# Where GpSimd issues the first two blocks of w_in in a fused attention and feed-forward kernel

## The chip, the cores and the metric

The kernel runs on one core of a Trainium2 chip. The metric is the device time of one execution in microseconds (us); a lower time is better. The core has a matrix engine (TensorE, in the profile PE, with its weight loads as PEld), VectorE (DVE), ScalarE (ACT), GpSimd (POOL) and SyncE (SP, which here only issues DMAs). GpSimd computes and also issues DMAs, in the order of its own instruction stream.

## The reference

Cosine attention over 8 batches of 12 heads, 448 positions and head size 64, followed by a two-layer network with an exact GELU:

```python
q_n = q / (np.linalg.norm(q, axis=-1, keepdims=True) + 1e-06)
k_n = k / (np.linalg.norm(k, axis=-1, keepdims=True) + 1e-06)
scores = np.matmul(q_n, k_n.transpose(0, 1, 3, 2)) / tau
scores = scores - np.max(scores, axis=-1, keepdims=True)
attn = np.exp(scores)
attn = attn / (np.sum(attn, axis=-1, keepdims=True) + 1e-09)
attn_out = np.matmul(attn, v)
...
x = attn_out.transpose(0, 2, 1, 3).reshape(B * S, H * D)
h = x @ w_in
g = 0.5 * h * (1.0 + erf(h * inv_sqrt2))
return g @ w_out
```

`x` is 3584 x 768, `w_in` 768 x 2048, `w_out` 2048 x 768. All inputs are float32 in DRAM; the products run in bf16.

## The kernel before

Heads are handled in quads of four: 24 quads in all, three for each batch. A quad's Q and K are loaded by `load_qk(g)` into one tile `qk` (four buffers), 448 KB for each of Q and K, on SP's queue. Quad 0 is split in two half quads, and so the work before the scores goes by units: unit 0 and unit 1 are the halves of quad 0, unit 2 is quad 1, unit 3 is quad 2, and so on.

For a unit u, `square` makes the squares (ScalarE for the first units, GpSimd later), `reduce` sums them on VectorE, `logs` and `roots` make the norms on ScalarE, `inverses` makes the reciprocals `rn` on VectorE, and `scale(u)` multiplies Q and K by them on GpSimd into the bf16 tile `qkb`. `transposes(u, i)` turns Q or K on TensorE, and `copies` moves the result to `qkT` on VectorE. Then, per quad, `scores` (TensorE), `exps` (ScalarE), `sums` of the exponentials (TensorE), `values` (TensorE, reads V) and `normalise` (VectorE), which writes the quad's columns of `x`.

V and both weights are loaded by GpSimd, whose DMAs turn float32 into bf16 on the way. `load_v(0)` brings quad 0's V, `load_v(1)` that of quads 1 and 2. `load_wi(i)` brings a block of `w_in`, as two DMAs, one for each half of the partitions: blocks 0 and 1 hold the rows that quads 0 and 1 meet, all columns; blocks 2 and 3 are the two column halves of the rows for quad 2. `load_wo(i)` brings a quarter of `w_out`. All of these go through one DMA queue (q0 in the profile); SP's loads and stores go through another (q1).

The first batch is written out by hand in `opening()`: there is no planner, and each engine works through its instructions in the order in which the calls stand there. `opening()` calls `load_wi(0)` behind `roots(0)`, ahead of `scale(0)`, and `load_wi(1)` behind `roots(2)`, ahead of `scale(2)`. GpSimd's stream up to the first squares is therefore: a one-element copy that waits for quad 0 (`late_copy`), load_v(0), load_wi(0), scale(0), scale(1), load_v(1), load_wi(1), scale(2), scale(3) Q, load_wi(2), scale(3) K, load_wi(3), squares of units 4 and 5, load_wo(0), load_wo(1). TensorE uses block 0 first in `mm(0, 4, 0, 2)`, between the last values of quad 2, then blocks 0 and 1 in `mm(0, 2, 0, 4)` and what follows, then blocks 2 and 3 in the products that finish each bank. `spin` issues products whose result nobody reads.

Of the kernel before, what the change touches and what calls it, by code (L numbers as in the profile page):

```python
# [16 lines left out]
def kernel(  # L17
# [109 lines left out]
    def load_qk(g, queue=None):  # L127
        b, n = divmod(g, NQ)
        t = qkp.tile([128, 2, 2, C, D], F32, tag="qk", name=f"qk{g}")
        qk_t[g] = t  # L130
        for s0, s1 in ((0, 1), (1, 2)) if g == 0 else ((0, 2),):
            for i, src in enumerate((q, k)):
                eng = queue or (nc.scalar if g == 0 and s0 == 0 and i == 1 else nc.sync)
                eng.dma_start(  # L134
                    out=t[:, i, s0:s1].rearrange("p s c d -> p s (c d)"),
                    in_=src[b, 4 * n + 2 * s0:4 * n + 2 * s1].rearrange(
                        "(s h) (p c) d -> (h p) s (c d)", h=2, c=C))
# [14 lines left out]
    def square(u, parts=None):  # L152
        g, s0, s1 = units[u]
        for eng, i in parts or ((nc.gpsimd, 0), (nc.gpsimd, 1)):
            if (g, i) not in sq_t:
                sq_t[g, i] = sqp.tile([128, 2, C, D], F32, tag="sq", name=f"sq{g}_{i}")
            sq, t = sq_t[g, i][:, s0:s1], qk_t[g][:, i, s0:s1]
            if eng is nc.scalar:
                eng.activation(sq, t, AF.Square)  # L159
            else:  # L160
                eng.tensor_tensor(sq, t, t, ALU.mult)  # L161
# [16 lines left out]
    def roots(n):  # L178
        ln = ln_t.pop(n)
        sr_t[n] = root2[2 if len(groups[n]) == 2 else n % 2][:, :math.prod(shapes[n])]  # L180
        nc.scalar.activation(sr_t[n][:, :, 0], ln.rearrange("p j i s c -> p (j i s c)"), AF.Exp, scale=0.5)
# [15 lines left out]
    def scale(u, parts=None):  # L197
        g, s0, s1 = units[u]
        n, j = place[u]
        rn = rn_t[n][:, j]  # L200
        if g not in qkb_t:
            qkb_t[g] = qkbp.tile([128, 2, C, 2, D], BF16, tag="qkb", name=f"qkb{g}")
        qkb, t = qkb_t[g], qk_t[g]
        for eng, i in parts or ((nc.gpsimd, 0), (nc.gpsimd, 1)):
            eng.tensor_tensor(  # L205
                qkb[:, i, :, s0:s1].rearrange("p c s d -> p s c d"), t[:, i, s0:s1],
                rn[:, i].to_broadcast([128, s1 - s0, C, D]), ALU.mult)
# [3 lines left out]
    def transposes(u, i=None):  # L211
        g, s0, s1 = units[u]
        qkb = qkb_t[g]
        if g not in qkT_t:
            qkT_t[g] = qkTp.tile([128, 2, C, 128], BF16, tag="qkT", name=f"qkT{g}")
        if i is None:
            nc.sync.dma_start_transpose(out=qkT_t[g].rearrange("p i c s -> p (i c) s"),
                                        in_=qkb.rearrange("p i c s d -> p (i c s d)"))
            return
        tp = tp_t[u, i] = mm_tile(f"tp{u}_{i}", (128, C, 128), BF16)  # L220
        for c in range(C):
            nc.tensor.transpose(tp[64 * s0:64 * s1, c, :], qkb[:, i, c, s0:s1].rearrange("p s d -> p (s d)"), ident)  # L222
# [10 lines left out]
    def scores(g, banks, p=None):  # L233
        qkT = qkT_t[g]
        if p is None:
            p = st_turn[0]
            st_turn[0] ^= 1
        st = pair(p, f"st{g}_{banks[0][1]}")
        for n, (s, c) in enumerate(banks):
            rows = slice(64 * s, 64 * (s + 1))  # L240
            for h in range(2):
                cols = slice(64 * h, 64 * (h + 1))
                nc.tensor.matmul(st[cols, n, :S], lhsT=qkT[rows, 1, c, cols], rhs=qkT[rows, 0, :, cols],  # L243
                                 start=True, stop=True, tile_position=(64 * s, 64 * h))
        st_t[g, banks[0]] = st

    def exps(g, banks):
        st = st_t.pop((g, banks[0]))
        if g not in all_t:
            all_t[g] = ptp.tile([128, C, 2, S], BF16, tag="pt", name=f"pt{g}")  # L250
        (s0, c0), (s1, c1) = banks
        pt = all_t[g][:, c0] if c0 == c1 else all_t[g][:, c0:c1 + 1, s0]
        nc.scalar.activation(pt, st[:, :, :S], AF.Exp, scale=inv_tau)  # L253
        for n, (s, c) in enumerate(banks):
            pt_t[g, s, c] = pt[:, n]
# [192 lines left out]
    def load_wi(i):  # L448
        n = min(i, NQ - 1)
        half = d_ff // 2  # L450
        cols = slice(0, d_ff) if n < NQ - 1 else slice((i - n) * half, (i - n + 1) * half)
        for s in range(2):
            nc.gpsimd.dma_start(
                out=wi[64 * s:64 * (s + 1), 2 * n:2 * n + 2, cols],
                in_=moe_w_in[:, cols].rearrange("(n s h d) f -> n s d h f", s=2, h=2, d=D)[n, s])
# [16 lines left out]
    def spin(n):  # L472
        ps = ps_mm.tile([128, 512], F32, tag=f"mm{turn[0]}", name="spin")
        for _ in range(n):
            nc.tensor.matmul(ps[:, :S], lhsT=ident, rhs=blank, start=True, stop=True)
# [48 lines left out]
    def opening():  # L524
# [14 lines left out]
        logs(0)  # L539
        reduce(1, Q)  # L540
        roots(0)
        load_wi(0)
        square(1, ((AC, K),))
        inverses(0)
        square(2, ((AC, Q),))
# [15 lines left out]
        copies(0, 0)  # L561
        square(3, ((AC, K),))
        scale(1, ((GP, 1),))
        load_qk(4)
        spin(1)
        transposes(1, 0)
# [5 lines left out]
        logs(2)  # L572
        scores(0, ((0, 2), (0, 3)))
        roots(2)
        load_wi(1)
        exps(0, ((0, 0), (0, 1)))
        inverses(2)
        copies(1, 1)
# [10 lines left out]
        spin(1)  # L589
        scores(0, ((1, 2), (1, 3)))  # L590
        scale(2, ((GP, 1),))
        load_qk(5)
        transposes(2, 0)
        exps(0, ((1, 2), (1, 3)))
# [763 lines left out]
    def open_fourth():  # L1358
        single.close()
        late[3] = ctx.enter_context(tc.tile_pool(name="ps_fourth", bufs=1, space=bass.MemoryType.PSUM))  # L1360

    opening()
    assert not todo_t, len(todo_t)
    first(2)
# [40 lines left out]
```

## Time and profile before

| what | us |
|---|---|
| runs of the kernel before | 392.3, 392.84, 399.61 |
| median | 392.84 |
| profiled execution | 393.7 |
| its span, first to last instruction | 391.9 |
| GpSimd busy | 246.9 |
| ScalarE busy | 270.3 |
| VectorE busy | 273.8 |

The span is what the profile shows; the profiled execution's own time holds 1.8 us around it. Times in rows are microseconds from the start of the span. A row of a timeline reads: start, duration, engine, line of the kernel, operation, output and inputs with their shapes, count, and in brackets how long the engine stood idle before it and whose result ended that. The line of a DMA issue shows how long the issuing engine took, not the transfer; for the transfer there is a time from issue to landing. A DMA queue's row gives the packets in a stretch, the megabytes, and the packets' time as a share of the 16 DMA engines.

### The profile page before, as it was taken

What the parts mean: (1) busy time and instruction counts of PE and PEld (TensorE: products, weight loads), DVE (VectorE), ACT (ScalarE), POOL (GpSimd) and SP (SyncE); (2) the same over time, 40 slices, a digit from 0 to 9 for tenths busy, and PEclk for the clock granted to TensorE, in tenths of its full rate; (3) what the DMA queues carried; (4) which work ended last, traced back from release to release, by engine and by line L of the source; (5) the groups of instructions that cost most, each with busy time, mean ns of one, the idle gap of its engine ahead of it and who ended that gap; (6) DMA issues with size and microseconds to landing.
All of it is one profiled execution on the core that took longest, in us unless ns stands there. A gap on an engine that the chain in (4) does not pass through costs nothing.

```text
span 391.9 us, 13170 instructions
## 1 busy us (share of the span) xinstructions
PE 384.0 (98%) x5820; PEld 236.8 (60%) x5820; DVE 273.8 (70%) x509; ACT 270.3 (69%) x391; POOL 246.9 (63%) x159
## 2 busy tenths in 40 slices
PE   7999998999999999999999999999999999999996
PEld 3444566655677656775566556775566655665674
DVE  4788248777668996889696896889685993670032
ACT  6895697758999967997577867997577646504200
POOL 4897911357999299969595694969596680910000
PEclk9999999999999999999999999999999999999999
DMA  7999999538798682879166590765034600130033
GB/s 269 263 262 228 203 191 295 197 65 190 190 230 268 114 203 81 184 137 259 41 131 152 131 247 3 185 118 129 3 90 75 156 11 2 43 82 2 2 83 82
DMA packets 64457, 54.85 MB, mean 140 GB/s; under 512 B 38672, under 2 KB 60304, under 8 KB 64400
## 3 DMA queue, kind: packets, MB, share of 16 engines
q1 hardware_dynamic: 54464, 41.79, 41.4%
q0 software_dynamic: 9552, 11.80, 18.2%
q8 instruction: 45, 0.74, 0.8%
q10 hardware_dynamic: 384, 0.43, 0.4%
q14 instruction: 12, 0.10, 0.1%
HBM read 45.61 MB, written 11.01 MB: 144 GB/s over the span
## 4 chain that ended last, share of the span: by engine, by line
PE 88%; DMA 3%; POOL 3%; DVE 2%; issue 1%; ACT 1%; SPq 1%; POOLq 0%; ACTq 0%
PE op L413 34%; PE hp L479 33%; PE st L243 8%; PE o L332 8%; DMA qk<-in_k_dram 2%; POOL qkb L205 2%; PE op L437 1%; PE sm L309 1%; DMA qkT<-qkb 1%; POOL sq L161 1%; PE tp L222 1%; SPq L134 1%; PE sm L318 1%; ACT pt L253 1%; DVE x L366 1%
## 5 line engine op out<-in xcount | busy, mean ns | idle before, releaser
L413 PE MATMUL op<-wo,g 64*64 64x384 bf16 x3456 | 167.4, 323 | 1.4 <-issue 1.4
L253 ACT ACTIVATE pt<-st 128x896 bf16<-128x896 f32 x168 | 147.6, 917 | 23.1 <-PE st L243 20.8
L479 PE MATMUL hp<-x,wi 128*128 128x448 bf16 x768 | 147.1, 353 | 0.0
L413 PEld LDWEIGHTS <-g 64*64 64x64 bf16 x3456 | 106.3, 107 | 42.5 <-issue 6.0
L479 PEld LDWEIGHTS <-wi 128*128 128x128 bf16 x768 | 74.2, 98 | 71.8 <-issue 3.2
L205 POOL TENSOR_TENSOR qkb<-qk,rn 128x896 bf16<-128x896 f32 (+1 forms) x49 | 80.3, 1663 | 46.2 <-DVE rn L189 38.2
L264 POOL TENSOR_TENSOR acc<-acc,pt 128x896 f32<-128x896 f32 x55 | 103.7, 1886 | 4.3
L422 DVE TENSOR_REDUCE ot<-op 128x384 f32<-128x768 f32 x50 | 47.3, 945 | 54.7 <-PE op L413 54.5
L1326 ACT ACTIVATE g<-hp 128x448 bf16<-128x448 f32 x96 | 46.2, 548 | 54.8 <-PE hp L479 54.8
L243 PE MATMUL st<-qkT 64*64 64x448 bf16 x672 | 63.1, 352 | 0.5 <-ACT pt L253 0.2
L169 DVE TENSOR_REDUCE nq<-sq 128x14 f32<-128x896 f32 (+1 forms) x50 | 50.4, 1037 | 12.0 <-ACT sq L159 6.5
L161 POOL TENSOR_TENSOR sq<-qk 128x896 f32<-128x896 f32 x16 | 26.6, 1685 | 31.0 <-DMA qk<-in_q_dram 17.5
L366 DVE TENSOR_TENSOR x<-o,rs 128x448 bf16<-128x448 f32 x48 | 27.8, 614 | 23.6 <-PE o L332 22.6
L332 PE MATMUL o<-pt,v 64*64 64x448 bf16 x672 | 40.0, 350 | 0.0
L276 DVE TENSOR_TENSOR acc<-acc,pt 128x896 f32<-128x896 f32 x30 | 33.0, 1099 | 1.0
L159 ACT ACTIVATE sq<-qk 128x896 f32<-128x896 f32 (+1 forms) x33 | 28.8, 901 | 3.3 <-DMA qk<-in_q_dram 2.3
L243 PEld LDWEIGHTS <-qkT 64*64 64x64 bf16 x672 | 23.4, 106 | 11.9 <-issue 4.2
L361 DVE STREAM_TRANSPOSE rs<-rc 128x448 f32<-128x448 f32 x48 | 28.1, 621 | 0.3
L264 POOL TENSOR_TENSOR acc<-pt 128x896 f32<-128x896 bf16 x11 | 20.6, 1876 | 11.1 <-ACT pt L253 11.1
L332 PEld LDWEIGHTS <-v 64*64 64x64 bf16 x672 | 21.4, 107 | 9.5 <-issue 0.5
L508 ACT ACTIVATE g<-hp 128x448 bf16<-128x448 f32 x32 | 15.5, 547 | 12.7 <-PE hp L479 12.7
L281 DVE TRANSPOSE_TENSOR_REDUCE sa<-acc 128x28 f32<-128x896 f32 x17 | 18.7, 1100 | 0.2
(53 smaller groups left out, 175.6 us busy)
## 6 DMA issues: line engine op xcount, KB each, us to landing
qk<-in_q_dram SPq DMA_DIRECT2D x23, 448.0 KB, 4.9
qk<-in_k_dram SPq DMA_DIRECT2D x23, 448.0 KB, 5.5
out_dram<-ot SPq DMA_DIRECT2D x48, 192.0 KB, 3.2
v<-in_v_dram POOLq DMA_DIRECT2D x7, 672.0 KB, 6.9
wo<-in_moe_w_out_dram POOLq DMA_DIRECT2D x4, 768.0 KB, 11.1
wi<-in_moe_w_in_dram POOLq DMA_DIRECT2D x4, 512.0 KB, 14.0
out_dram<-ot SPq DMA_DIRECT2D x12, 96.0 KB, 2.2
wi<-in_moe_w_in_dram POOLq DMA_DIRECT2D x4, 256.0 KB, 14.4
```

The lines of the kernel that those rows point to most:

```text
L169: nc.vector.tensor_reduce(nq_t[n][:, j, i], sq_t[g, i][:, s0:s1], mybir.AxisListType.X, ALU.add)
L205: eng.tensor_tensor(qkb[:, i, :, s0:s1].rearrange("p c s d -> p s c d"), t[:, i, s0:s1], rn[:, i].to_broadcast([128, s1 - s0, C, D]), ALU. ...
L243: nc.tensor.matmul(st[cols, n, :S], lhsT=qkT[rows, 1, c, cols], rhs=qkT[rows, 0, :, cols], start=True, stop=True, tile_position=(64 * s, 6 ...
L253: nc.scalar.activation(pt, st[:, :, :S], AF.Exp, scale=inv_tau)
L264: nc.gpsimd.tensor_tensor(acc_t[g], all_t[g][:, 0] if c == 1 else acc_t[g], all_t[g][:, c], ALU.add)
L276: nc.vector.tensor_tensor(acc_t[g], acc_t[g], all_t[g][:, c], ALU.add)
L332: nc.tensor.matmul(bank_t[g, h][cols, :S], lhsT=v_t[g][rows, s, c, :], rhs=pt_t[g, s, c][rows], start=(c == 0), stop=(c == C - 1), tile_po ...
L366: nc.vector.tensor_tensor(x_t[b][:, 2 * n + h, :], bank_t.pop((g, h))[:, :S], rs_t.pop((g, h)), ALU.mult)
L413: nc.tensor.matmul(ps[cols, r, :NH], lhsT=g_t[sb][rows, kf, t * 128 + 64 * c:t * 128 + 64 * (c + 1)], rhs=wo[rows, kf, ni * NH:(ni + 1) * NH],
L422: nc.vector.tensor_reduce(part, ps[:, :, :NH].rearrange("p r d -> p d r"), mybir.AxisListType.X, ALU.add)
L479: nc.tensor.matmul(t, lhsT=wi[:, kd, m * 128:(m + 1) * 128], rhs=x_t[b][:, kd, :], start=(kd == 0), stop=(kd == KD - 1))
L1326: nc.scalar.activation(g_t[sb][:, m, hf * S:(hf + 1) * S], hps.pop(m), AF.Gelu)
```

## The change

Two calls in `opening()` are moved; nothing is added or taken away. `load_wi(0)` goes behind `scale(1)`, the last scale of the two half quads, and stands ahead of `load_v(1)` on GpSimd. `load_wi(1)` goes behind the K half of `scale(2)`, which is quad 1's scale, and stands ahead of `scale(3)`, then `load_wi(2)`. The order of the transfers within q0 stays: v(0), w_in 0, v(1), w_in 1, w_in 2, w_in 3.

```diff
         reduce(1, Q)
         roots(0)
-        load_wi(0)
         square(1, ((AC, K),))
         inverses(0)
...
         square(3, ((AC, K),))
         scale(1, ((GP, 1),))
+        load_wi(0)
         load_qk(4)
...
         scores(0, ((0, 2), (0, 3)))
         roots(2)
-        load_wi(1)
         exps(0, ((0, 0), (0, 1)))
...
         scores(0, ((1, 2), (1, 3)))
         scale(2, ((GP, 1),))
+        load_wi(1)
         load_qk(5)
         transposes(2, 0)
```

## The prediction

> **What bounds it now.** I read the page first, then the same engines over four-microsecond stretches, then the timelines of GpSimd, VectorE, ScalarE and TensorE up to 40 us, and at last the DMA queues microsecond by microsecond with each transfer's time to landing.
>
> ```profile
> PE 384.0 (98%) x5820; PEld 236.8 (60%) x5820; DVE 273.8 (70%) x509; ACT 270.3 (69%) x391; POOL 246.9 (63%) x159
> DMA  7999999538798682879166590765034600130033
> PE 88%; DMA 3%; POOL 3%; DVE 2%; issue 1%; ACT 1%; SPq 1%; POOLq 0%; ACTq 0%
> ```
>
> TensorE bounds the program: 384.0 of 391.9 us, 88% of the chain that ended last. The DMA line shows the other side: from the second to the seventh slice (9.8 us each) it stands at 9. There transfers can decide who is late. A stretch inside says the same:
>
> ```profile
> 32.00:36.00 4.00, 4.00 (x29) 2.00 (x22) 3.41 (x8) 1.83 (x3) 1.83 (x2) 1.00 1.12 227
> ```
>
> The columns are PE, PEld, DVE, ACT and POOL busy, the clock, the DMA share and GB/s: the DMA share is over 1.0, TensorE is busy throughout and its clock is full.
>
> **The edit on GpSimd.** GpSimd's rows, in order, are the queue that the change reorders; the last row is SP's, the issue of qk3's K half:
>
> ```profile
> 5.77 0.88 POOL L146 DMA_DIRECT2D v<-in_v_dram  x1
> 6.65 1.21 POOL L453 DMA_DIRECT2D wi<-in_moe_w_in_dram  x2
> 7.86 1.86 POOL L205 TENSOR_TENSOR qkb<-qk,rn 128x448 bf16<-128x448 f32 x2
> 10.08 1.83 POOL L205 TENSOR_TENSOR qkb<-qk,rn 128x448 bf16<-128x448 f32 x2 [0.37 <-DVE rn L189]
> 11.86 0.83 POOL L146 DMA_DIRECT2D v<-in_v_dram  x1
> 12.68 1.21 POOL L453 DMA_DIRECT2D wi<-in_moe_w_in_dram  x2
> 13.87 3.37 POOL L205 TENSOR_TENSOR qkb<-qk,rn 128x896 bf16<-128x896 f32 x2
> 18.27 1.69 POOL L205 TENSOR_TENSOR qkb<-qk,rn 128x896 bf16<-128x896 f32 x1 [1.03 <-PE tp L222]
> 19.91 1.25 POOL L453 DMA_DIRECT2D wi<-in_moe_w_in_dram  x2
> ...
> 5.07 0.80 SPq L134 DMA_DIRECT2D qk<-in_k_dram  x1
> ```
>
> Each load_wi call here issues two DMAs in 1.21 to 1.25 us. Part by part:
>
> Taking load_wi(0) out at 6.65 lets scale(0) (the pair at 7.86) start up to 0.6 us sooner, as soon as rn0 is there. This is worth nothing, because the next pair, scale(1) at 10.08, waits for VectorE:
>
> ```profile
> 8.56 1.08 DVE L169 TENSOR_REDUCE nq<-sq 128x14 f32<-128x896 f32 x1 [0.67 <-ACT sq L159]
> 9.76 0.24 DVE L189 RECIPROCAL rn<-se 128x14 f32<-128x14 f32 x1
> 17.81 0.33 DVE L189 RECIPROCAL rn<-se 128x28 f32<-128x28 f32 x1
> 11.07 0.58 PE L222 MATMUL tp<-ident,qkb 128*64 128x128 bf16 x7 [0.19 <-POOL qkb L205]
> 11.56 0.95 ACT L159 ACTIVATE sq<-qk 128x896 f32<-128x896 f32 x1 [0.66 <-DMA qk<-in_k_dram]
> 19.24 12.07 ACT L253 ACTIVATE pt<-st 128x896 bf16<-128x896 f32 x14 [0.16 <-PE st L243]
> ```
>
> rn1 is ready at 9.76 + 0.24 = 10.00, after a reduction that waited for ScalarE, and the transposes at 11.07 stand ahead of the first scores on TensorE. The cover is 10.08 - 9.72 = 0.37 us of idle GpSimd that becomes 0.95. Were that cover gone, the edit would gain up to 0.6 us. ScalarE's last idle time before its exponentials, 0.66 us at 11.56, is for qk2's K half; whether that lands sooner is a question for the DMA rows below, and they say no.
>
> load_wi(0) now stands at 11.9 and load_wi(1) leaves 12.68, so between scale(1) and scale(2) there is again one load_wi and one load_v: 11.86 + 1.21 + 0.83 = 13.9, and scale(2) starts at 13.87 as before. load_qk(4), on SP's queue, is only moved past in the text: it waits for scale(1) as before. But load_v(1) is now issued at 11.9 + 1.2 = 13.1.
>
> load_wi(1) now starts when scale(2) ends, 13.87 + 3.37 = 17.24, and holds GpSimd until 18.45. scale(3)'s Q half behind it could start at 18.27 (rn3: 17.81 + 0.33 = 18.14). So scale(3) starts 0.2 us later, and all GpSimd work behind it (load_wi(2), scale(3)'s K half, load_wi(3), four squares, load_wo) moves by that. TensorE waits for exactly this scale:
>
> ```profile
> 20.02 0.39 PEld L222 LDWEIGHTS <-qkb 128*128 128x128 bf16 x7 [0.43 <-POOL qkb L205]
> 25.87 0.74 PE L332 MATMUL o<-pt,v 64*64 64x448 bf16 x12
> 32.17 13.42 PE L479 MATMUL hp<-x,wi 128*128 128x448 bf16 x70
> 60.73 0.68 PE L413 MATMUL op<-wo,g 64*64 64x384 bf16 x11 [1.23 <-issue]
> ...
> ```
>
> 18.27 + 1.69 = 19.96, and the weights of the transposes load at 20.02. The next scores stand behind them, and ScalarE runs 14 exponentials from 19.24 without a gap, so nothing hides it: term one is +0.2 us.
>
> **The edit on the DMA queue.** GpSimd's transfers go through one queue, q0, and SP's loads through q1. The first fence is the microsecond from 9, then from 10, 14 and 20, 36 and the two from 86:
>
> ```profile
> q1 hardware_dynamic: 232, 0.39, 104.4%
> ...
> q0 software_dynamic: 88, 0.08, 47.9%
> ...
> q0 software_dynamic: 41, 0.17, 82.5%
> q1 hardware_dynamic: 41, 0.07, 21.1%
> ...
> q0 software_dynamic: 106, 0.09, 57.9%
> q1 hardware_dynamic: 108, 0.18, 55.6%
> ...
> q0 software_dynamic: 139, 0.21, 114.7%
> ...
> q0 software_dynamic: 221, 0.20, 91.0%
> ```
>
> The columns are packets, MB and share. From 9 to 10 only q1 has a row; q0's first packets run in the microsecond from 10, although v(0) was issued at 5.77. Where both have work they alternate packet for packet (41 and 41, 106 and 108), so a w_in packet takes most of the time. At 36 q1 is empty and q0 has everything. Now the landings, issue plus time to landing:
>
> ```profile
> v<-in_v_dram POOLq DMA_DIRECT2D x1, 224.0 KB, 7.6
> ...
> v<-in_v_dram POOLq DMA_DIRECT2D x1, 448.0 KB, 13.3
> ...
> wi<-in_moe_w_in_dram POOLq DMA_DIRECT2D x1, 512.0 KB, 15.6
> wi<-in_moe_w_in_dram POOLq DMA_DIRECT2D x2, 512.0 KB, 17.1
> ...
> wi<-in_moe_w_in_dram POOLq DMA_DIRECT2D x1, 256.0 KB, 13.9
> wi<-in_moe_w_in_dram POOLq DMA_DIRECT2D x2, 256.0 KB, 14.4
> ...
> qk<-in_k_dram SPq DMA_DIRECT2D x1, 448.0 KB, 14.9
> ```
>
> In order: v(0), v(1), w_in's second block (one transfer, then the mean of its two: the other took 2 x 17.1 - 15.6 = 18.6), its third block (the other 14.9), and qk3's K half. v(1) lands at 11.86 + 13.3 = 25.2 us; TensorE reads it at 25.87. w_in's second block lands at 12.68 + 0.6 + 18.6 = 31.9; the third product of the run at 32.17 reads it, at 32.17 + 2 x 0.19 = 32.55. The third block, issued at 19.91, lands at 20.5 + 14.9 = 35.4 and is read at the 23rd product, 32.17 + 22 x 0.19 = 36.35. q0 is a line in which nothing is early: the slacks are 0.7, 0.65 and 0.95 us.
>
> What the change does to that line: v(0)'s 256 packets (224 KB by 896 bytes) at 88 to 106 a microsecond from 10.0 end near 12.5, and before the change w_in's first block followed at once. qk2's K half had passed by then, which is why nothing is gained at 11.56. Now that block is issued only at 11.9. How long q0 takes to start again I bound by two rows: 4.2 us (5.77 to 10.0, behind a full q1), and 1.6 us with an idle DMA:
>
> ```profile
> 84.44 0.88 POOL L146 DMA_DIRECT2D v<-in_v_dram  x1
> ...
> ```
>
> (84.44, first packets in the stretch from 86, none in the two microseconds before). So q0 runs again between 13.5 and 16.1, and lags by 1.0 to 3.6 us. In between: at 5.77 q1 had qk1, qk2 and qk3 queued, 6 x 256 packets; at 11.9 it has most of qk3's two halves (its K half, issued at 5.07, lands only at 20.0). That is a third, so I take a third of the way: 1.6 + 2.6 / 3 = 2.5 us, a start at 14.4 and a lag of 1.9 us.
>
> A price from elsewhere: the Trainium skill, "DMA: Bandwidth & Descriptors", Specifications, gives about 1 us to the first byte of a DMA issued from GpSimd. By it, as an estimate, q0 would start at 12.9 and the lag be 0.4 us, and the sum would be +0.2 us, not +1.2. The trace disagrees in both places where it can be read, 4.2 and 1.6 us.
>
> v(1) follows w_in's first block, against a q1 that still holds qk4, so the lag stays whole: it lands at 27.1 (26.2 to 28.8). It is wanted at 25.87 + 0.2 = 26.1: term two is a stall of 1.0 us (0.1 to 2.7). Behind the waiting product on TensorE stand the next scores, and for those ScalarE waits. w_in's later blocks: what q0 loses, q1 has gained, since the DMA stays full, and q0 catches up once q1 is empty before 36. At the second block the lag is at most 1.9, the slack 0.65 plus the 1.2 by which TensorE is late: 0.05 short at worst, taken as nothing. From 32 us TensorE runs at its rate (70 products in 13.42 us), so a delay reaches the end unless the 1.23 us gap before 60.73 takes some.
>
> Sum: 0 + 0.2 + 1.0 = +1.2 us. The profiled execution took 393.7 us (span 391.9 and 1.8 around it), so 394.9. The median of the runs, 392.84, lies 0.86 below that execution; on its scale the forecast is 394.0 us, 0.3% slower, which is no change that can be told: what a measurement of this kernel can tell is about 2%, 7.9 us.
>
> **Rivals.** One: q0 restarts fast, in 1.6 us or less. The lag is at most 1.0, v(1) lands at 26.2 or sooner, and only scale(3)'s 0.2 us is left, which the gap at 59.5 can swallow; if TensorE's later arrival also closes that gap, which falls into a full stretch of DMA, it is -1.2 us. That is 391.6 to 393.1. For it: at 11.9 q1 holds less than at 5.77. Against: the wait of 4.2 us is this queue's only one in the same loaded stretch. By the figure of the Trainium skill's page "DMA: Bandwidth & Descriptors" this would be the case. Chance 0.27.
>
> Two, slower than the forecast and than before: q0 restarts as slowly as at 5.77, and q1's gain gives nothing back, so that all of q0 lags 3.6 us. v(1) lands at 28.8 and stalls 2.7; the second block lands at 35.5 against 32.55 + 2.9 = 35.45. Together +3.0 us: 395.8 by the median, 396.7 by the profiled execution. It decides from a restart of 3 us on. For it: qk4, issued beside the block, may get in first. Chance 0.18.
>
> Three: the reorder gains, because scale(0) or q1's earlier loads do release something. qk5 would land sooner, for which GpSimd's squares wait near 36; but TensorE then has 70 products queued and wants nothing of it. At most the 0.6 us of the first edit: 392.2. Chance 0.05.
>
> The forecast has 0.45. What is left, 0.05, is a price that no row shows; one of the three runs before stands at 399.61, 1.7% above the middle one.
>
> **Numbers.** The range takes the ends of rivals one and two: 391.6 to 396.8. No case reaches 7.9 us; the unexplained part and the spread of the three runs give 0.06 to slower by over 2%, 0.03 to faster, 0.91 to between.
>
> **What would show it.** After: scale(1) starts within 0.1 us of 10.08; ScalarE's square of qk2's K half still starts near 11.56; scale(2) starts near 13.9 and scale(3) near 18.5; qk3 and qk4 land sooner by microseconds; q0 has a hole between 12.5 and about 14.4; v(1) lands near 27.1 and the products on v at 25.87 show a gap of about 1 us; the 70 w_in products begin near 33.4. I am wrong if v(1) lands before 26, if q0 has no hole, or if TensorE's delay at 32 us is not found at the end.

## The result, and the profile after

| | runs | median us | lowest to highest |
|---|---|---|---|
| before | 20 | 393.58 | 392.04 to 400.2 |
| changed | 20 | 395.32 | 393.5 to 399.19 |

The ratio changed to before is 1.0063, with a 95% interval of 1.0039 to 1.0087: 0.6% slower, about 2.5 us. Executions more than 1.5% above the fastest of their kernel are left out of the ratio, which takes six of before (398.13 and more) and none of the changed kernel, although the mean granted clock of TensorE (the share of its full clock that it was given) was under 0.998 in nine of the latter. To keep apart what the change costs and what the clock costs, I sort executions below by their mean granted clock and call 0.998 and above full clock.

The profiled execution of the changed kernel, 398.85 us with a span of 397.1, is one of those with a lowered clock. From its page, engines, clock and DMA share in 40 slices, and the chain that ended last:

```profile
PE 388.7 (98%) x5820; PEld 236.5 (60%) x5820; DVE 273.8 (69%) x509; ACT 270.8 (68%) x391; POOL 247.0 (62%) x159
PEclk9579999999999999999999999999999999999999
DMA  8999999716999856679336690666033610120033
PE 90%; ACT 3%; DVE 2%; issue 2%; POOL 1%; POOLq 0%; DVEq 0%
```

The clock line has a 5 and a 7 where before had 9. The stretches (PE, PEld, DVE, ACT, POOL busy, clock, DMA share, GB/s) and TensorE's timeline of the same execution say when and behind what:

```profile
8.00:12.00 4.00, 2.20 (x24) 1.48 (x23) 2.93 (x6) 3.15 (x5) 2.31 (x3) 0.99 1.09 343
12.00:16.00 4.00, 4.00 (x22) 1.39 (x21) 2.78 (x6) 3.11 (x5) 3.49 (x5) 0.50 1.09 329
...
24.00:28.00 4.00, 4.00 (x59) 1.81 (x59) 1.93 (x4) 2.87 (x4) 4.00 (x5) 0.80 1.15 272
```

```profile
8.98 0.55 PE L222 MATMUL tp<-ident,qkb 128*64 128x128 bf16 x7
11.01 0.35 PE L475 MATMUL spin<-g,ident 128*128 128x448 bf16 x1 [1.49 <-DVE qkT L227]
```

TensorE stood idle for 1.49 us before 11.01, then ran at half clock from about 12 to 26 us. In this execution everything behind is late anyhow, so v(1) is never waited for, and the profile hides the change's own cost. It takes a second profile of the same kernel, at full clock, to see it; that is the second experiment.

### The profile page after: what moved, and what is told of

It reads as the page before. It is cut to its first block, busy times and chain, and to the rows that moved or that the text cites. A ratio compares the mean times of both kernels' runs of the same rounds, so it can differ in the third digit from the quotient of the medians.

```text
span 397.1 us, 13170 instructions
## 1 busy us (share of the span) xinstructions
PE 388.7 (98%) x5820; PEld 236.5 (60%) x5820; DVE 273.8 (69%) x509; ACT 270.8 (68%) x391; POOL 247.0 (62%) x159
## 3 DMA queue, kind: packets, MB, share of 16 engines
HBM read 45.61 MB, written 11.01 MB: 143 GB/s over the span
## 4 chain that ended last, share of the span: by engine, by line
PE 90%; ACT 3%; DVE 2%; issue 2%; POOL 1%; POOLq 0%; DVEq 0%
PE hp L479 37%; PE op L413 32%; PE st L243 9%; PE o L332 8%; ACT pt L253 2%; PE sm L309 2%; DVE acc L269 1%; PE op L437 1%; PE tp L222 1%; POOL qkb L205 1%; PE sm L318 1%; PE spin L475 0%; ACT sq L159 0%; ACT L487 0%; DVE sa L281 0%
## 5 line engine op out<-in xcount | busy, mean ns | idle before, releaser
L413 PEld LDWEIGHTS <-g 64*64 64x64 bf16 x3456 | 105.0, 107 | 42.1 <-issue 4.8
L243 PE MATMUL st<-qkT 64*64 64x448 bf16 x672 | 65.6, 363 | 0.2
L243 PEld LDWEIGHTS <-qkT 64*64 64x64 bf16 x672 | 23.0, 108 | 13.1 <-issue 5.8
## 6 DMA issues: line engine op xcount, KB each, us to landing
wi<-in_moe_w_in_dram POOLq DMA_DIRECT2D x4, 512.0 KB, 11.6
```

Of the source, the lines that this page charges most:

```text
L413: nc.tensor.matmul(ps[cols, r, :NH], lhsT=g_t[sb][rows, kf, t * 128 + 64 * c:t * 128 + 64 * (c + 1)], rhs=wo[rows, kf, ni * NH:(ni + 1) * NH],
```

## The experiments

**Both kernels again.** No edit. The first asks what the clock has to do with the spread of before, the second for a profile of the changed kernel at full clock. In what was expected, theory A holds that the time is lost to a lowered TensorE clock, theory B that it is lost to transfers and waits that moved.

> The kernel before, unchanged, for the granted clock of each of its executions. Theory A (halved clock in the first 30 us costs whole executions 3 to 6 us): executions over 397 us show a mean granted clock under 0.99, those at 392 to 394.7 one of 0.998 or more. Theory B (only transfers and waits move): the clock does not sort the executions.

> The changed kernel, unchanged, for a second profile and more executions. Theory A: about half of the executions have a mean clock under 0.998 and stand 2 to 5 us above the rest; if A is all, the rest stand at the 393.0 us of the kernel before. Theory B (v(1) lands about 1 us after it is wanted, and the third scale starts 0.2 us later): the executions at full clock stand 1.2 us above the kernel before, near 394.2.

Executions by mean granted clock, all sets of the study together (count and mean us):

| kernel | full clock | 0.99 to 0.998 | under 0.99 |
|---|---|---|---|
| before (105) | 78, 393.27 | 12, 396.82 | 15, 399.11 |
| changed (32) | 19, 394.38 | 5, 396.58 | 8, 398.35 |

The clock does sort the executions (theory A's half): nearly all that stand above 396 us have a clock under 0.998, in both kernels. Theory B's half holds as well: at full clock the changed kernel is 1.1 us slower than before (plus or minus 0.4, two standard errors). In the second set alone (8 executions at full clock against 29 of before) it was 1.5 us slower, and the repeated kernel before stood 0.4 us above those 29, so differences of 0.4 us between single sets tell nothing. A lowered clock came in four of its 12 executions, not in half of them.

The second profile of the changed kernel, span 393.7, clock 0.999. GpSimd's timeline first:

```profile
7.28 1.83 POOL L205 TENSOR_TENSOR qkb<-qk,rn 128x448 bf16<-128x448 f32 x2 [0.74 <-DVE rn L189]
10.50 1.83 POOL L205 TENSOR_TENSOR qkb<-qk,rn 128x448 bf16<-128x448 f32 x2 [1.39 <-DVE rn L189]
12.28 1.26 POOL L453 DMA_DIRECT2D wi<-in_moe_w_in_dram  x2
13.52 0.79 POOL L146 DMA_DIRECT2D v<-in_v_dram  x1
...
18.00 1.25 POOL L453 DMA_DIRECT2D wi<-in_moe_w_in_dram  x2
19.27 1.70 POOL L205 TENSOR_TENSOR qkb<-qk,rn 128x896 bf16<-128x896 f32 x1
```

Then the queue rows of q0 in the microseconds from 13, 14 and 15 (packets, MB, share), and v(1)'s time from issue to landing:

```profile
q0 software_dynamic: 1, 0.00, 0.1%
...
q0 software_dynamic: 4, 0.02, 9.5%
...
q0 software_dynamic: 42, 0.17, 88.7%
...
v<-in_v_dram POOLq DMA_DIRECT2D x1, 448.0 KB, 15.4
```

And TensorE, with the chain of waits by engine from the page:

```profile
26.65 0.38 PE L243 MATMUL st<-qkT 64*64 64x448 bf16 x4
28.97 0.76 PE L332 MATMUL o<-pt,v 64*64 64x448 bf16 x12 [1.94 <-DMA v<-in_v_dram]
...
35.27 13.41 PE L479 MATMUL hp<-x,wi 128*128 128x448 bf16 x70
...
61.30 1.63 PE L413 MATMUL op<-wo,g 64*64 64x384 bf16 x36
...
PE 86%; DMA 4%; ACT 3%; DVE 2%; issue 2%; POOL 2%; POOLq 0%; DVEq 0%
```

q0 is empty from 13 to about 15; v(1) lands at 13.52 + 15.4 = 28.9, and TensorE waits 1.94 us for it, a wait that neither of the two profiles of before has at this place. The last TensorE row is read further below. The profile of the repeated kernel before, span 390.7, serves as the partner (TensorE's and GpSimd's timelines, and v(1), issued at 11.62):

```profile
19.70 0.56 PE L222 MATMUL tp<-ident,qkb 128*128 128x128 bf16 x7
...
25.55 0.74 PE L332 MATMUL o<-pt,v 64*64 64x448 bf16 x12
...
59.66 0.68 PE L413 MATMUL op<-wo,g 64*64 64x384 bf16 x11 [0.49 <-issue]
...
17.95 1.69 POOL L205 TENSOR_TENSOR qkb<-qk,rn 128x896 bf16<-128x896 f32 x1 [0.96 <-PE tp L222]
...
v<-in_v_dram POOLq DMA_DIRECT2D x1, 448.0 KB, 13.4
```

**More idle products on TensorE.** To fill the hole before 11 us in the changed kernel:

```diff
         inverses(1)
-        spin(1)
+        spin(5)
         transposes(0, 0)
```

> The changed kernel with four more idle products (0.19 us each) on TensorE ahead of the transposes of unit 0's Q. Theory A: TensorE's idle time between 9.5 and 11 us shrinks from 1.5 to about 0.75 us and the executions under a clock of 0.99 become rare; the mean falls by 1 to 2 us. Theory B: no execution at full clock gets faster, the median stays at 394.2 or above; what A takes off comes from the slow executions alone.

Of 12 executions none had a clock under 0.99, ten were at full clock, at 394.67, so nothing was won there: both theories' halves again. The mean over all executions went from the changed kernel's 395.72 to 395.31 only, not down by 1 to 2 us. The profiled execution, 396.11 us, has a mean clock of 0.995, and the stall of v(1) too (it landed at 12.8 + 15.2 = 28.0). TensorE's timeline, GpSimd's, and the stretch behind the stall:

```profile
19.88 0.56 PE L222 MATMUL tp<-ident,qkb 128*128 128x128 bf16 x7 [0.21 <-POOL qkb L205]
28.02 0.76 PE L332 MATMUL o<-pt,v 64*64 64x448 bf16 x12 [2.12 <-DMA v<-in_v_dram]
...
18.11 1.71 POOL L205 TENSOR_TENSOR qkb<-qk,rn 128x896 bf16<-128x896 f32 x1
...
28.00:32.00 4.00, 3.98 (x44) 1.50 (x44) 1.77 (x4) 1.83 (x2) 4.00 (x4) 0.62 1.09 211
```

Here the stall of 2.12 us is itself followed by half clock, from 28.9 to 32.3 us.

**v(1) ahead of w_in's first block.**

```diff
         scale(1, ((GP, 1),))
+        load_v(1)
         load_wi(0)
...
-        load_v(1)
         transposes(1, 1)
```

> The changed kernel with v(1) issued ahead of w_in's first block, so that v(1) is 256 w_in packets earlier in the queue. Theory B: v(1) lands near 20 us instead of 27, the executions at full clock fall by 1.0 us to 393.2; w_in's first block lands about 5 us later, still before 30. Theory A: executions with a lowered clock are as common as in the changed kernel, about half.

v(1) landed at 13.1 + 7.6 = 20.7, and the eight executions at full clock stand at 392.90: 1.5 us under the changed kernel and level with before. Three of 12 were under 0.99, the profiled one among them, so its TensorE is late anyhow. That TensorE doesn't wait for v(1) at full clock either is seen in a profile of the same order with four more idle products (below; clock 1.0, v(1) landed at 11.6 + 7.7 = 19.3):

```profile
25.94 0.74 PE L332 MATMUL o<-pt,v 64*64 64x448 bf16 x12
```

One reorder of two neighbours takes the whole loss at full clock away, as theory B has it.

**One block alone.** Of the change's two moves only the second, and only the first:

```diff
# the second block alone, against before
-        load_wi(1)
         exps(0, ((0, 0), (0, 1)))
...
         scale(2, ((GP, 1),))
+        load_wi(1)
```

> Only w_in's second block is moved; the first stays ahead of scale(0). Theory B (the lateness of v(1) is the cost, and it comes from the first block's move): v(1) lands near 25 us as in the kernel before, TensorE does not wait for it, and the executions at full clock stand at 393.2, within 0.3 of the kernel before. If the second block's move had a part in the loss, they stand 0.5 us or more above it.

```diff
# the first block alone, against before
         roots(0)
-        load_wi(0)
...
         scale(1, ((GP, 1),))
+        load_wi(0)
         load_qk(4)
```

> Only w_in's first block is moved; GpSimd then issues three transfers (3.3 us) between scale(1) and scale(2), so scale(2) starts 1.3 us later than before. Theory B: v(1) lands near 28.5 us, TensorE, late by 1.2 us already, waits for it about 1 us; the executions at full clock stand 1.2 to 2 us above the kernel before, 394.4 to 395.2. If the first block's move alone cost nothing, they stand 1.2 above at most, all of it from scale(2).

The second block alone: 392.96 at full clock (10 of 12), no loss, and v(1) landed at 13.3 + 11.2 = 24.5. The first alone: 394.81 (6 of 12), 1.6 us above the before of the same set, give or take 1.0. The time is as expected, but it can't tell the wait for v(1) from the 1.2 us that scale(2) alone was expected to cost, and its profile doesn't show a wait of about 1 us: v(1) landed at 13.2 + 15.0 = 28.2, and the weights of its products waited 0.19 us for it. In that execution (393.1 us span, clock 0.995) the clock had fallen to half at 17.1 us and made TensorE late already. That the loss comes with the first block's move rests on the kernel with the second block alone, which loses nothing. The rows of the first-block kernel are TensorE's, the stretch in which the clock fell, and the weight load that waited:

```profile
14.27 0.57 PE L243 MATMUL st<-qkT 64*64 64x448 bf16 x4 [0.49 <-ACT pt L253]
17.00 0.91 PE L222 MATMUL tp<-ident,qkb 128*128 128x128 bf16 x7 [0.55 <-POOL qkb L205]
...
16.00:20.00 4.00, 3.45 (x25) 1.54 (x23) 1.93 (x4) 2.52 (x5) 3.32 (x3) 0.63 1.04 234
...
28.30 0.33 PEld L332 LDWEIGHTS <-v 64*64 64x64 bf16 x12 [0.19 <-DMA v<-in_v_dram]
```

The second-block kernel's profile has a lowered clock as well, and is telling for that: scale(0) stands there where before has it, and TensorE still has a hole before the clock falls:

```profile
9.67 0.55 PE L222 MATMUL tp<-ident,qkb 128*64 128x128 bf16 x7
12.01 0.35 PE L475 MATMUL spin<-g,ident 128*128 128x448 bf16 x1 [1.79 <-DVE qkT L227]
```

**v(1) behind both blocks.** The kernel before, with v(1) behind w_in's second block:

```diff
         roots(2)
         load_wi(1)
+        load_v(1)
...
-        load_v(1)
         transposes(1, 1)
```

> The kernel before with v(1) issued behind w_in's second block instead of ahead of it, nothing else moved: v(1)'s lateness alone, and about twice as much of it as in the changed kernel. Theory B: v(1) lands 5 to 6 us later than the 25.2 us of the kernel before, near 31, TensorE waits 4 to 5 us for it, and the executions stand 3 to 5 us above the kernel before. Theory A adds that so long a wait lets the clock fall in nearly every execution, mean clock 0.99 to 0.997. If v(1)'s landing is not what is paid for, the time stays within 0.5 us.

The five executions took 399.34 to 401.7 us, the mean 6.6 us above the full-clock executions of before in the same set (393.52), all at a clock of 0.990 to 0.991. v(1) landed at 12.6 + 18.6 = 31.2; TensorE's wait and the stretches:

```profile
31.26 1.34 PE L332 MATMUL o<-pt,v 64*64 64x448 bf16 x12 [5.34 <-DMA v<-in_v_dram]
...
27.00:30.00 3.00, 0.00 (x0) 0.00 (x0) 1.31 (x2) 0.00 (x0) 3.00 (x3) 0.62 1.15 281
30.00:33.00 3.00, 1.74 (x20) 0.93 (x24) 0.00 (x0) 0.00 (x0) 2.03 (x3) 0.50 1.13 240
```

Nothing but the order of v(1) and w_in's second block was changed, so a late v(1) is paid for. The price came out larger than the 3 to 5 us expected; the wait itself is 5.34 us, and the clock was lowered in every execution.

**v(1) early, in the old place of w_in's first block.**

```diff
         roots(0)
+        load_v(1)
...
-        load_v(1)
         transposes(1, 1)
```

> v(1) is issued in the place that w_in's first block had, ahead of scale(0), and both blocks stay where the change puts them. Theory B: v(1) lands before 18 us, q0 has no hole before 15 us, TensorE does not wait for v(1), and the executions at full clock stand at 392.9 or a little less. If the loss came from scale(3) or from w_in's blocks being late, they stay at 394.

This one went against theory B. v(1) landed at 6.4 + 11.0 = 17.4 and was not waited for, yet the nine executions at full clock stand at 394.36, as slow as the changed kernel. Its profile has a wait for w_out and a longer idle time near 60 us than before (1.23 and 0.49):

```profile
53.09 1.17 PE L413 MATMUL op<-wo,g 64*64 64x384 bf16 x24 [0.28 <-DMA wo<-in_moe_w_out_dram]
...
60.95 0.68 PE L413 MATMUL op<-wo,g 64*64 64x384 bf16 x11 [1.56 <-issue]
```

TensorE arrives early and stands later. So a loss of this size can also arise without any wait for v(1); what the gap near 60 us waits for is read below. Why w_out comes later there was not settled.

**The idle products without the change, and with v(1) first.** The same `spin(5)` in the kernel before, and in the version with v(1) ahead of the first block, twice.

> v(1) ahead of w_in's first block, and four more idle products ahead of the transposes of unit 0's Q. Theory A (TensorE's idle time before 11 us lets the clock fall in part of the executions): executions under a clock of 0.99, 3 of 12 without the products, become 0 or 1 of 12, and the executions at full clock stay at 392.9. If the idle time has no part in it, they stay at about a quarter.

> The kernel before with the four more idle products ahead of the transposes of unit 0's Q. Theory A: executions under a clock of 0.99 (11 of 82 executions of the kernel before with a known clock) become 0 of 12 or 1, executions at full clock stay near 393.2. If the products have no part in it, one or two of 12 are under 0.99.

> The version with v(1) ahead of w_in's first block and four more idle products once more, beside the kernel before: theory A expects again no execution under a clock of 0.99, and a mean over all executions of 393.6, 0.5 to 1.4 us under that of the kernel before; the executions of both at full clock within 0.5 us of each other.

| kernel | full clock | 0.99 to 0.998 | under 0.99 |
|---|---|---|---|
| v(1) first, idle products (24) | 23, 393.47 | 1, 397.12 | 0 |
| before, idle products (12) | 9, 393.96 | 2, 398.29 | 1, 399.59 |

With the first block moved, the products go with fewer lowered clocks: 11 of 44 executions under 0.99 without them (changed kernel and v(1) first), 0 of 36 with them. In the kernel before they show nothing: 1 of 12 against 15 of 105. The version with v(1) first and the products has the best mean over all its executions in both of its sets (393.60 against 395.04 of before, and 393.65 against 394.49), but its ratios, 1.0005 (0.9977 to 1.0033) and 1.0006 (0.9981 to 1.0031), show no gain over before. No version was shown to beat the kernel before.

## Why the prediction was right, step by step

**The direction and the size.** Forecast +1.2 us; at full clock it is +1.1 (0.4 either way). The median, 395.32, lies in the range. What the ratio has beyond that, some 1.4 us, goes with the lowered clock of the executions that stay in it, which the prediction had not priced: in that set the eleven changed executions at full clock average 394.25, all twenty 395.72. The direction and its reason were right; that the size fits so closely is luck, since two errors cancel, below.

**scale(0) earlier is worth nothing.** Right: rn0 released it at 7.28, and scale(1) still waited for rn1. But scale(1) did not stay within 0.1 us of 10.08: it stood at 10.50 and 10.57. qk1's Q half, issued at 2.15 as before, needed 5.8 and 5.9 us to land where before it had needed 5.4; as the second-block kernel had scale(1) at 11.57 with scale(0) in its old place, and the changed kernel with idle products at 9.76, this varies from execution to execution, and nothing shows it to be the change's. What I did not see is that TensorE's transposes and idle products move forward with scale(0) and leave a hole behind them. Whether that makes the clock fall more often than before (8 of 32 against 15 of 105) the runs do not settle; a hole of 1.79 us arises without it.

**Term one, +0.2 us for scale(3).** Right: 18.11 against 17.95 on GpSimd, 19.88 against 19.70 on TensorE, with the mark of the wait.

**Term two, v(1) late.** The mechanism was right, and this is the term that was mis-sized. The hole in q0 was forecast from 12.5 to 14.4 and measured from about 13 to 15; the restart took 2.6 us from the issue at 12.28, where I had taken 2.5. By the about 1 us of the Trainium skill's "DMA: Bandwidth & Descriptors", Specifications, it would, as an estimate, have come at 13.3, and the trace disagrees. But I let v(1)'s landing lag by the 1.9 us of the queue. Between the two profiles whose scale(1) starts within 0.1 us of each other, the one with idle products and the repeated before, it lagged from 11.62 + 13.4 = 25.0 to 28.0, 3.0 us. So the stall was 1.94 and 2.12 us, not 1.0; rival two's 2.7 was nearer. What rival two gave as its reason, a restart as slow as 4.2 us, did not happen. q1 gained what q0 lost, as forecast: in the second profile qk3's K half landed in 10.3 us instead of 14.9.

**What I left out on the other side.** The prediction said that the gap before 60.73 might take some of the delay and put no number to it. In the second profile of the changed kernel the 70 w_in products begin at 35.27, not at 33.4: 3.1 us behind before and 3.4 behind its repeat, since scale(1) and with it all that follows came later there too. Behind the gap only 1.7 and 2.7 us of that are left (62.95 against 61.28 and 60.21), and the spans differ by 1.8 and 3.0. So the gap took 1.4 and 0.7 us. The prediction had called itself wrong if TensorE's delay at 32 us was not found at the end; it was found there only in part. Before, TensorE stands idle there for 1.23 us (0.49 in the repeat); the changed kernel's row at 61.30 has all 36 products with no idle time. As an estimate, 0.2 + 2.1 less about 1 us is 1.3, near the measured +1.1.

The rows are those of before, its repeat, the changed kernel, and before with four more idle products; the last two are the instruction queue, q8, from 58 to 59 us, in before and in the one with idle products:

```profile
58.20 1.30 PE L413 MATMUL op<-wo,g 64*64 64x384 bf16 x25
...
61.28 1.94 PE L413 MATMUL op<-wo,g 64*64 64x384 bf16 x40
...
60.21 1.94 PE L413 MATMUL op<-wo,g 64*64 64x384 bf16 x40
...
62.95 1.79 PE L413 MATMUL op<-wo,g 64*64 64x384 bf16 x40
...
58.69 1.13 PE L413 MATMUL op<-wo,g 64*64 64x384 bf16 x21
61.31 0.84 PE L413 MATMUL op<-wo,g 64*64 64x384 bf16 x15 [1.49 <-issue]
...
q8 instruction: 1, 0.02, 7.5%
...
q8 instruction: 1, 0.02, 7.3%
```

What ends the gap is not v, w_in or w_out, as far as the profiles tell. It comes after the 25th of these 36 products, and with four more products ahead of it in TensorE's stream it comes after the 21st: it goes with the place in the stream of instructions. One packet of instructions passes on q8 each time, and TensorE goes on 2.4 to 2.6 us later: 58.15 and 60.73 in before, 57.15 and 59.66 in the repeat, 58.80 and 61.31 with idle products, 58.60 and 60.95 in the kernel with v(1) early, where the packet comes later than in either profile of before and the gap is longer. In the changed kernel the packet passes at 58.65, and TensorE reaches that place only at about 62.3. So the gap looks like a wait for instructions, for which a late TensorE has no need and an early one gains nothing. No run moved that packet by itself, so this is read from the profiles and not shown by experiment.

**The costs at nothing.** Right: in no profile does a w_in product show a wait for w_in, and the 70 products take 13.4 us everywhere. That the later blocks caught up fits what was worked out, although TensorE was later than forecast and so asked less of them.

**The clock.** I read it as full from one profiled execution and had no price for a stall's second effect. Executions of the changed kernel with a clock under 0.99 stand 4.0 us above those at full clock (398.35 against 394.38), those of 0.99 to 0.998 stand 2.2 above.

## What to carry to other kernels

On a queue that is never empty, moving one transfer back moves every transfer behind it. Ask first which of those is wanted soonest: here two neighbouring calls swapped undid the loss. One profiled execution shows one state of the clock: where the spread of the times is larger than the effect, sort the executions by granted clock before comparing, and get a profile of each kind. An idle gap further down can set a floor: part of a delay ahead of it costs nothing, and part of a gain ahead of it brings nothing. Ask what ends the gap.

## What the runs showed of the hardware

TensorE's granted clock halved after idle times much shorter than I had thought harmless: 1.49 us in the changed kernel, 1.79 in the second-block kernel, 2.12 behind v(1). But the length of the last idle time does not decide it: one of 1.94 us went by without it, and in the first-block kernel the clock fell at 17.1 us behind idle times of only 0.49 and 0.55 us. The Trainium skill, "TensorE: Matmul & The Clock Gate", Part 1, lets the clock fall after an idle window of about 3.4 us that runs freely; these holes are shorter, with TensorE only partly busy around them, so the number as a limit for a gap is not borne out here.

The clock stayed at half for 3.4 us (17.05 to 20.46 in the first-block kernel, 28.9 to 32.3 behind the stall of 2.12), 6.8 us (27.7 to 34.6 with v(1) behind both blocks) or 13.6 us (11.9 to 25.6 in the changed kernel), close to one, two and four times the same length. Half of 13.6 us lost in 397 makes a mean clock of 0.983, half of 6.8 makes 0.991, half of 3.4 makes 0.996. The mean clocks of the lowered executions stand close to these values and to 0.987, which three such lengths would make.

A transfer can lag more at its landing than at its first packet. In the pair of profiles above (idle products and repeated before) q0's first w_in packets came about 2.0 us later (14.3 against 12.3), but v(1), behind them in the queue, landed 3.0 us later, though the queue's order had not changed. Why was not settled.
